# Attention and expert kernel: relu of q moved from GpSimd to VectorE one batch ahead, v scaling shared by ScalarE and VectorE, early expert reads without the last batch's writes among their dependencies

## The chip, the cores and the metric

The kernel runs on one core of a Trainium2 chip. The core has five engines, each with a queue of its own that is worked off in order: TensorE (PE in the profile, with its weight loads as PEld), VectorE (DVE), ScalarE (ACT), GpSimd (POOL) and SyncE (SP, which here only issues DMAs). Sixteen DMA engines move data between DRAM and the on-chip memory SBUF; matmul results land in PSUM. The metric is the device time in microseconds (us); less is better.

## The reference

A linear attention with cosine weights, followed by a mixture of experts with one expert per token. There are 8 batches of 8 heads, 576 positions and 64 dimensions; the attention result, turned to 4608 tokens of 512 features, is the experts' input.

```python
theta = np.pi / 2.0 * pos / S                       # S = 576
phi = lambda x: concat([relu(x) * cos(theta), relu(x) * sin(theta)])   # on the last axis
kv  = einsum('bhsf,bhsd->bhfd', phi(k), v);  z = sum(phi(k), axis=2)
attn = einsum('bhsf,bhfd->bhsd', phi(q), kv) / (einsum('bhsf,bhf->bhs', phi(q), z) + 1e-06)
x = attn.transpose(0, 2, 1, 3).reshape(4608, 512)
logits = x @ w_gate;  expert = argmax(logits);  gate = softmax(logits)[expert]   # 8 experts
# the first 1152 tokens of each expert are kept, in token order
out[i] = gate[i] * (relu(x[i] @ w1[expert]) @ w2[expert])   # w1: 512 x 1024, w2: 1024 x 512; others 0
```

## The kernel before

A batch's 576 positions are cut into `NJ` = 4 chunks of 128 and a tail of 64 (`NC` = 5); its 8 heads go in 4 pairs. The first part loops over `it` = 0 to 8 (`B` = 8) and works on three batches at a time. Each stage returns a list of small steps, and `run` merges the lists into one program: a list is given with the stretch (lo, hi) of the iteration over which its steps are spread evenly, and the steps of all lists are sorted by that place. This fixes the order in every engine's queue.

- `load(it + 1)` issues the six DMAs of the next batch on SP: k, v and q, each as a main part and a tail. k and v have two buffers, q (`qm`, `qt`) has one, so the next q can be loaded only when the relu of the present one has read it.
- `stage_a(it)`: `relu_k` on ACT; `relu_q(w)`, four instructions on POOL that write the rectified q of a head pair into `qr` with the heads reordered, and two more for the tail, `qrt`; `scale_v(c, t)`, which multiplies chunk c of v by the cosine (t = 0) or sine (t = 1) table into `vs`, on DVE for the four chunks and on ACT for the tail; `q_pair(w)`, which turns a pair of `qr` on PE (`q_ps`) and copies it to `rq` on ACT; `kv_pair(w)`, the products of k and scaled v on PE (`kv_ps`), with a copy to `kvt` on ACT and one to `kva` on DVE for every two pairs; then `transp` and `gates`, which fold the router's weights into `kva` (`t_ps`, `g_ps`).
- `stage_p(it - 1)`: ten units, each four products of `rq` and `kva` on PE (`p_ps`, two buffers), a scaled copy on ACT (`tmp`) and a multiply-add on DVE (`num`).
- `stage_r(it - 2)`: the router, about twenty small DVE instructions in one chain with an Exp on ACT (`ex`) and the counting product on PE (`c_ps`, which needs `oh`); it makes the row numbers `slot_i` and the factors `rden`. Then `emit(c)` multiplies the token rows (`xg`; chunks 1 and 3 on POOL, the rest on DVE), and `scatter(c)` writes them by indirect DMAs on POOL to `xd`, a DRAM buffer sorted by expert.
- `w1_piece(0, e)`: one expert's first half of w1 (`w1a`), a DMA on POOL near the end of an iteration. Seven of the eight go one per iteration, and the eighth beside the last.

After the loop `table_a` works out, on DVE, where the first `NA` = 24 blocks of 128 rows lie. The second part runs over 43 blocks: `fetch` reads a block from `xd` by a transposing DMA on SP (`xT`, ten buffers, and `ids`), `up` multiplies with w1 (`h_ps`), `turn` transposes, `down` multiplies with w2 (`y_ps`), and rows go to the output by an indirect DMA on POOL. The first seven blocks run `up` with `w1a` alone beside the router of the last batch (`stage_r(7)`, `table_b`); the loads of `w1b` (second half of w1) and `w_sb` (w2) follow on POOL behind that router's scatters. `down` of block 0 comes 17 blocks behind its `up` and needs all of `w_sb`.

A read of `xd` depends on the writes that stand ahead of it in the program. Writes and reads can be declared free of a group: the scatters of the last batch and the zero rows of `table_b` are free of reads that were put into "early reads" ahead of them.

## Time and profile before

| | us |
|---|---|
| median of 3 runs | 501.11 (497.33 to 501.25) |
| profiled execution, its own time | 497.33 |
| its span, first to last instruction | 495.5 |
| PE busy | 349.4 (71%) |
| POOL busy | 192.1 (39%) |
| DVE busy | 185.3 (37%) |
| ACT busy | 170.6 (34%) |

The profile is of one execution. Its span lies 1.8 us below the time of the same execution. Busy times are sums over stages with different limits, so none of them says by itself what bounds the kernel; the order of time and the waits do. An engine's wait is given with the instruction that ended it ("<-POOL qr"). PEclk is TensorE's granted clock, as a share of the full one.

### The profile page before, as it was taken

Reading aid. Unit: us, or ns where it says so; the run is one execution under the profiler, and the core shown is the slowest. Engines: PE = TensorE matmul, PEld = TensorE weight load, DVE = VectorE, ACT = ScalarE, POOL = GpSimd, SP = SyncE. Lnnn points to the kernel's source line nnn. Section 1 sums busy time; section 2 is a strip of 40 time slices with the busy share of each in tenths; the row PEclk is TensorE's granted clock in tenths of the full one; section 3 lists DMA queues with packets and bytes.
Section 4 is the critical chain, followed back from the end, with each engine's and each line's share of the span. In section 5 each row is a group of like instructions: output and inputs, shape, how many; then the busy total and the mean of one; then the engine's idle time right before and its main releaser. Section 6 shows DMA issues by size and latency. Waiting matters only on the chain.

```text
span 495.5 us, 8167 instructions
## 1 busy us (share of the span) xinstructions
PE 349.4 (71%) x2672; PEld 219.3 (44%) x2672; DVE 185.3 (37%) x544; ACT 170.6 (34%) x319; POOL 192.1 (39%) x205
## 2 busy tenths in 40 slices
PE   0099969495867859587406022987499999999994
PEld 0066657374645647366303011443155555555441
DVE  1203456445474635456836200231023232223222
ACT  1046574433645435343202000452033434333110
POOL 3163604908375573916524722000022222222544
PEclk9998979777887978787658555998799999999998
DMA  2968372828467381404173999999955433111221
GB/s 47 331 198 270 81 224 68 234 78 259 119 200 179 112 247 30 82 1 83 41 114 82 183 198 201 190 187 197 158 117 113 102 97 111 72 64 64 92 91 54
DMA packets 91559, 66.55 MB, mean 134 GB/s; under 512 B 46077, under 2 KB 88061, under 8 KB 91520
## 3 DMA queue, kind: packets, MB, share of 16 engines
q0 software_dynamic: 22000, 30.96, 28.9%
q1 hardware_dynamic: 68368, 34.01, 28.0%
q10 hardware_dynamic: 1152, 1.05, 0.7%
q8 instruction: 24, 0.39, 0.3%
q14 instruction: 15, 0.12, 0.1%
HBM read 61.92 MB, written 17.06 MB: 159 GB/s over the span
## 4 chain that ended last, share of the span: by engine, by line
PE 31%; issue 24%; POOL 19%; DMA 15%; SPq 4%; DVE 3%; ACT 2%; another core or an unknown queue 1%; POOLq 1%; ACTq 0%; DVEq 0%
PE h_ps L660 13%; PE y_ps L681 9%; POOL qr L217 7%; POOL xd L493 5%; DMA xT<-xd 5%; DMA out_dram<-y,ix 4%; DMA qm<-in_q_dram 4%; PE ht_ps L671 3%; PE kv_ps L291 2%; POOL xg L485 2%; PE p_ps L329 2%; DMA ids<-xd 2%; POOL qrt L222 2%; POOL out_dram L693 1%
## 5 line engine op out<-in xcount | busy, mean ns | idle before, releaser
L662 ACT ACTIVATE h<-h_ps 128x512 bf16<-128x512 f32 x86 | 51.4, 597 | 126.4 <-PE h_ps L660 116.4
L681 PE MATMUL y_ps<-w_sb,hT 128*128 x344 | 81.1, 384 | 8.8 <-DMA w_sb<-in_moe_w_dram 6.5
L329 PE MATMUL p_ps<-kva,rq 64*128 64x146 f32 (+1 forms) x640 | 77.0, 356 | 3.9 <-ACT kva L315 2.4
L672 DVE COPY hT<-ht_ps 128x512 bf16<-128x512 bf16 x86 | 33.2, 420 | 119.8 <-PE ht_ps L671 107.9
L660 PEld LDWEIGHTS <-xT 128*128 128x128 bf16 x344 | 34.4, 101 | 98.3 <-DMA xT<-xd 40.3
L660 PE MATMUL h_ps<-w1a,xT 128*128 x172 | 47.2, 399 | 43.1 <-DMA xT<-xd 43.0
L336 DVE SCALAR_TENSOR_TENSOR num<-p_ps,sintab,tmp 128x292 f32<-128x292 f32 (+1 forms) x80 | 41.6, 520 | 84.6 <-ACT tmp L334 83.6
L693 POOL DMA_INDIRECT out_dram<-y,ids x24 | 23.4, 977 | 121.6 <-DVE y L687 84.0
L262 PE MATMUL q_ps<-ident,qr 128*128 128x128 f32 x128 | 30.0, 377 | 53.3 <-POOL qr L217 53.3
L329 PEld LDWEIGHTS p_ps<-kva,rq 64*128 64x128 f32 (+1 forms) x640 | 56.6, 215 | 15.9 <-issue 5.6
L217 POOL TENSOR_SCALAR qr<-qm 128x512 f32<-128x512 f32 x32 | 46.8, 1485 | 30.5 <-DMA qm<-in_q_dram 30.1
L485 POOL TENSOR_TENSOR xg<-num,rden 128x512 bf16<-128x512 f32 x16 | 21.0, 1313 | 95.4 <-DVE rden L478 95.3
L660 PE MATMUL h_ps<-w1b,xT 128*128 x172 | 47.3, 401 | 15.0 <-DMA ids<-xd 14.9
L334 ACT ACTIVATE tmp<-p_ps,costab 128x292 f32<-128x292 f32 (+1 forms) x80 | 40.0, 502 | 48.8 <-PE p_ps L329 47.1
L681 PEld LDWEIGHTS <-hT 128*128 128x128 bf16 x344 | 32.9, 99 | 45.0 <-issue 12.2
L493 POOL DMA_INDIRECT xd<-xg,slot_i x40 | 42.8, 1069 | 10.0 <-issue 8.2
L262 PEld LDWEIGHTS q_ps<-ident,qr 128*128 128x128 f32 x128 | 19.3, 188 | 60.8 <-POOL qr L217 56.6
L291 PE MATMUL kv_ps<-vs,km 128*64 128x130 f32 x512 | 39.9, 303 | 0.0
L264 ACT COPY rq<-q_ps 128x512 f32<-128x512 f32 x32 | 18.6, 581 | 45.8 <-PE q_ps L262 45.7
L291 PEld LDWEIGHTS kv_ps<-vs,km 128*64 128x64 f32 x512 | 31.2, 150 | 5.8 <-issue 1.0
L687 DVE COPY y<-y_ps 128x512 f32<-128x512 f32 x22 | 15.2, 692 | 45.9 <-PE y_ps L681 24.8
L671 PEld LDWEIGHTS <-h 128*128 128x128 bf16 x344 | 24.3, 101 | 14.1 <-issue 2.7
(140 smaller groups left out, 339.7 us busy)
## 6 DMA issues: line engine op xcount, KB each, us to landing
km<-in_k_dram SPq DMA_DIRECT2D x8, 1024.0 KB
vm<-in_v_dram SPq DMA_DIRECT2D x8, 1024.0 KB
qm<-in_q_dram SPq DMA_DIRECT2D x8, 1024.0 KB
w_sb<-in_moe_w_dram POOLq DMA_DIRECT2D x8, 1024.0 KB
w1a<-in_moe_w_dram POOLq DMA_DIRECT2D x8, 512.0 KB
w1b<-in_moe_w_dram POOLq DMA_DIRECT2D x8, 512.0 KB
xd<-zrow ACTq DMA_DIRECT2D x8, 128.5 KB
kt<-in_k_dram SPq DMA_DIRECT2D x8, 128.0 KB
```

Source lines behind the costliest of these rows:

```text
L217: nc.gpsimd.tensor_scalar(out=qr[:, w, :, :, :].rearrange("p j o d -> p o j d"), in0=qm[:, u * HB + r:u * HB + r + 3:2, :, :], scalar1=0.0 ...
L262: nc.tensor.transpose(out=q_ps[:, j, :], in_=qr[:, w, j, :, :].rearrange("p o d -> p (o d)"), identity=ident[:])
L291: nc.tensor.matmul(out=kv_v[o * D:(o + 1) * D, w % 2, :, :], lhsT=lhsT, rhs=rhs, start=(c == 0), stop=(c == NC - 1))
L329: nc.tensor.matmul(out=p_ps[0:rows, o, r, 0:2 * KW], lhsT=rq[o * D:(o + 1) * D, 2 * u + r, c * P:c * P + rows], rhs=kva[o * D:(o + 1) * D, ...
L334: nc.scalar.activation(out=tmp[0:rows], in_=p_v[0:rows, :, 0:KW], func=ACT.Copy, scale=costab[0:rows, c:c + 1])
L336: nc.vector.scalar_tensor_tensor(out=num[0:rows, c, u * HB:(u + 1) * HB, :], in0=p_v[0:rows, :, KW:2 * KW], scalar=sintab[0:rows, c:c + 1] ...
L493: si = nc.gpsimd.indirect_dma_start(out=xd[:, :], out_offset=bass.IndirectOffsetOnAxis(ap=slot_i[0:rows, c:c + 1], axis=0), in_=xg[0:rows, ...
L660: nc.tensor.matmul(out=h_ps[:], lhsT=bl["xT"][:, g, :], rhs=w1h[n][:, bass.ds(e1, 1), g, :], start=(g == 0), stop=(g == G - 1))
L662: nc.scalar.activation(out=h[:], in_=h_ps[:], func=ACT.Relu)
L671: nc.tensor.transpose(out=t_ps[:, f, :], in_=bl["h", n][:, f * P:(f + 1) * P], identity=identb[:])
L672: nc.vector.tensor_copy(out=bl["hT"][:, n * (FB // 2):(n + 1) * (FB // 2), :], in_=t_ps[:])
L681: nc.tensor.matmul(out=y_ps[:], lhsT=bl["hT"][:, f, :], rhs=w2_sb[:, bass.ds(e2, 1), f, :], start=(f == 0), stop=(f == FB - 1))
```

## The change

The relu of q leaves `stage_a` and becomes a function of its own, `relu_q(b)`: four DVE instructions, two for the main part (one for each head of a pair, 1024 elements per partition) and two for the tail (256 elements). In iteration `it` it is run for batch `it + 1`, spread from 0.7 to 0.95; batch 0's stands ahead of the loop. v scaling of chunks 2 and 3 goes from DVE to ACT, and the list of scalings is written in another order. The `kva` copy goes from DVE to ACT. `stage_r` is spread over 0 to 0.85 in place of 0 to 1, and over 0 to 0.5 in the last iteration, where `table_a`, now in two pieces, takes 0.5 to 1. The eight `w1a` pieces are all issued by iteration 7, two each in iterations 6 and 7. The first 24 fetches are declared free of the "late rows": the last batch's scatters and the zero rows.

```diff
+    def relu_q(b):
+        if b >= B:
+            return []
+        qm, qt = loaded[b]["q"]
+        qr = io1.tile([P, 4, NJ, 2, D], FP32, name="qr", tag="qr")
+        qrt = io1.tile([D, 4, 2, D], FP32, name="qrt", tag="qrt")
+        qrs[b] = (qr, qrt)
+        def main(o):
+            def f():
+                nc.vector.tensor_scalar(
+                    out=qr[:].rearrange("p (u r) j o d -> p u (r j) o d", u=2)[:, :, :, o, :],
+                    in0=qm[:].rearrange("p (u o r) j d -> p u o (r j) d", u=2, o=2)[:, :, o, :, :],
+                    scalar1=0.0, scalar2=None, op0=ALU.max)
+            return f
...
+        return [main(0), main(1), tail(0), tail(1)]
...
-        def relu_q(w):
-            def f():
-                u, r = w // 2, w % 2
-                nc.gpsimd.tensor_scalar(
-                    out=qr[:, w, :, :, :].rearrange("p j o d -> p o j d"),
-                    in0=qm[:, u * HB + r:u * HB + r + 3:2, :, :], scalar1=0.0, scalar2=None, op0=ALU.max)
...
+        qr, qrt = qrs.pop(b)
...
-                if c == NJ:
+                if c >= 2:
                     nc.scalar.activation(out=vs[0:rows, c, :, t, 0:D], in_=src, func=ACT.Copy,
...
         elem += [relu_k(0)]
-        for c in range(NC):
-            elem += [scale_v(c, 0), scale_v(c, 1)]
-            if c == 1:
-                elem.append(relu_k(1))
+        elem += [scale_v(0, 0), scale_v(2, 0), scale_v(0, 1), scale_v(2, 1), relu_k(1), scale_v(1, 0),
+                 scale_v(3, 0), scale_v(1, 1), scale_v(3, 1), scale_v(4, 0), scale_v(4, 1)]
...
-                    nc.vector.tensor_copy(out=kva[:, w - 1:w + 1, :, 0:D + 1], in_=kv_v)
+                    nc.scalar.copy(out=kva[:, w - 1:w + 1, :, 0:D + 1], in_=kv_v)
...
                 if b == B - 1:
                     free_of(si, "early reads")
+                    member(si, "late rows")
...
             free_of(zi, "early reads")
+            member(zi, "late rows")
...
     load(0)
+    run((relu_q(0), 0.0, 1.0))
     for it in range(B + 1):
         streams = []
         if it < B:
             load(it + 1)
-            elem, rls, qs, kvst = stage_a(it)
-            streams += [(elem, 0.0, 0.5), (rls, 0.0, 0.3), (qs, 0.1, 0.5), (kvst, 0.45, 1.0)]
+            elem, qs, kvst = stage_a(it)
+            streams += [(elem, 0.0, 0.5), (qs, 0.0, 0.45), (kvst, 0.45, 1.0)]
+        if it + 1 < B:
+            streams.append((relu_q(it + 1), 0.7, 0.95))
         if 1 <= it:
             streams.append((stage_p(it - 1), 0.05, 0.97))
         if 2 <= it:
-            streams.append((stage_r(it - 2, ps_a, "a"), 0.0, 1.0))
-            streams.append(([w1_piece(0, it - 2)] + ([w1_piece(0, 7)] if it == B else []), 0.9, 1.0))
+            streams.append((stage_r(it - 2, ps_a, "a"), 0.0, 0.85 if it < B else 0.5))
+            if it < B:
+                lots = {6: (4, 5), 7: (6, 7)}.get(it, (it - 2,))
+                streams.append(([w1_piece(0, e) for e in lots], 0.9, 1.0))
+            else:
+                streams.append((table_a(), 0.5, 1.0))
         run(*streams)
-    table_a()
...
         if i < NA:
-            member(ti, "early reads")
-            member(di, "early reads")
+            for x in (ti, di):
+                free_of(x, "late rows")
+                member(x, "early reads")
```

What this moves in the engines' queues is shown at three places. The first is POOL in an iteration of the middle, from the router's first write of one batch (the token numbers in `xg`) on. Before:

```order
L217 TENSOR_SCALAR qr<-qm 128x2x4x64 x4
L222 TENSOR_SCALAR qrt<-qt 64x2x2x64 x2
L485 TENSOR_TENSOR xg<-num_186,rden 128x512
L493 DMA xd<-xg,slot_i 37888x514
L485 TENSOR_TENSOR xg<-num_186,rden 128x512
L493 DMA xd<-xg,slot_i 37888x514 x3
L508 DMA w1a<-in_moe_w_dram 128x4x512
L493 DMA xd<-xg,slot_i 37888x514
L374 TENSOR_SCALAR xg<-tok_i 128x5
```

And now:

```order
L384 TENSOR_SCALAR xg<-tok_i 128x5
L495 TENSOR_TENSOR xg<-num_186,rden 128x512
L503 DMA xd<-xg,slot_i 37888x514
L495 TENSOR_TENSOR xg<-num_186,rden 128x512
L503 DMA xd<-xg,slot_i 37888x514 x4
L519 DMA w1a<-in_moe_w_dram 128x4x512
```

The six relu instructions are gone from the queue, and the w1 piece stands behind the last scatter.

The second place is ACT in the first half of an iteration of the middle, up to the second scaling of v's tail (`vs<-vt,sintab`). Before:

```order
L264 COPY rq<-q_ps 128x512
L230 ACTIVATE km<-km 128x1024
L233 ACTIVATE kt<-kt 64x512
L334 ACTIVATE tmp<-p_ps,costab 128x292
L264 COPY rq<-q_ps 128x512
L334 ACTIVATE tmp<-p_ps,costab 128x292
L264 COPY rq<-q_ps 128x512
L242 ACTIVATE vs<-vt,costab 64x8x64
L273 COPY rq<-qt_ps 128x4x64
L334 ACTIVATE tmp<-p_ps,costab 128x292
L242 ACTIVATE vs<-vt,sintab 64x8x64
```

And now:

```order
L274 COPY rq<-q_ps 128x512
L242 ACTIVATE km<-km 128x1024
L245 ACTIVATE kt<-kt 64x512
L344 ACTIVATE tmp<-p_ps,costab 128x292
L254 ACTIVATE vs<-vm,costab 128x8x64
L274 COPY rq<-q_ps 128x512
L344 ACTIVATE tmp<-p_ps,costab 128x292
L254 ACTIVATE vs<-vm,sintab 128x8x64
L283 COPY rq<-qt_ps 128x4x64
L254 ACTIVATE vs<-vt,costab 64x8x64
L344 ACTIVATE tmp<-p_ps,costab 128x292
L254 ACTIVATE vs<-vt,sintab 64x8x64
```

Two scalings of v's chunk 3 have come in between the q copies; those of chunk 2 stand likewise further ahead.

The third place is DVE near the end of an iteration of the middle, from the sixth `num` on. Before:

```order
L336 SCALAR_TENSOR_TENSOR num_184<-p_ps,sintab,tmp 128x292
L478 TENSOR_TENSOR rden<-rden,gate 128x40
L485 TENSOR_TENSOR xg<-num_186,rden 128x512
L336 SCALAR_TENSOR_TENSOR num_184<-p_ps,sintab,tmp 128x292
L485 TENSOR_TENSOR xg<-num_186,rden 128x512
L295 COPY kva<-kv_ps 128x4x65
L336 SCALAR_TENSOR_TENSOR num_184<-p_ps,sintab,tmp 64x292
L485 TENSOR_TENSOR xg<-num_186,rden 64x512
L336 SCALAR_TENSOR_TENSOR num_184<-p_ps,sintab,tmp 64x292
```

And now:

```order
L346 SCALAR_TENSOR_TENSOR num_186<-p_ps,sintab,tmp 128x292
L495 TENSOR_TENSOR xg<-num_184,rden 128x512 x2
L346 SCALAR_TENSOR_TENSOR num_186<-p_ps,sintab,tmp 128x292
L214 TENSOR_SCALAR qr<-qm 128x16x64
L346 SCALAR_TENSOR_TENSOR num_186<-p_ps,sintab,tmp 128x292
L495 TENSOR_TENSOR xg<-num_184,rden 64x512
L214 TENSOR_SCALAR qr<-qm 128x16x64
L346 SCALAR_TENSOR_TENSOR num_186<-p_ps,sintab,tmp 64x292
L222 TENSOR_SCALAR qrt<-qt 64x4x64 x2
L346 SCALAR_TENSOR_TENSOR num_186<-p_ps,sintab,tmp 64x292
```

The next batch's relu of q stands between the last four `num`, and the `kva` copy is gone.

## Rows read from the trace of the kernel before

**Rows 1.** The page's chain that ended last, shares of the span by line.

```profile
PE h_ps L660 13%; PE y_ps L681 9%; POOL qr L217 7%; POOL xd L493 5%; DMA xT<-xd 5%; DMA out_dram<-y,ix 4%; DMA qm<-in_q_dram 4%; PE ht_ps L671 3%; PE kv_ps L291 2%; POOL xg L485 2%; PE p_ps L329 2%; DMA ids<-xd 2%; POOL qrt L222 2%; POOL out_dram L693 1%
```

**Rows 2.** Busy time by step; columns: us, then PE, PEld, DVE, ACT, POOL, PEclk, DMA, GB/s.

```profile
41.32:61.38 20.06, 18.94 (x193) 14.19 (x193) 8.93 (x20) 12.61 (x26) 8.11 (x8) 0.91 0.61 180
61.38:85.85 24.47, 20.23 (x205) 15.71 (x205) 14.70 (x44) 14.21 (x28) 4.95 (x4) 0.86 0.47 145
85.85:115.75 29.90, 22.35 (x205) 17.07 (x206) 15.58 (x45) 13.06 (x27) 17.06 (x16) 0.77 0.56 157
115.75:143.21 27.46, 19.73 (x205) 15.13 (x205) 14.96 (x45) 12.96 (x27) 16.63 (x15) 0.81 0.61 169
...
198.10:227.60 29.50, 21.28 (x212) 16.41 (x211) 15.72 (x47) 13.35 (x29) 17.53 (x16) 0.83 0.20 40
```

**Rows 3.** Order of time in step 4; start, us, engine, line; idle before in brackets.

```profile
120.83 5.84 POOL L217 TENSOR_SCALAR qr<-qm 128x512 f32<-128x512 f32 x4
...
122.37 1.12 PE L262 MATMUL q_ps<-ident,qr 128*128 128x128 f32 x4 [5.62 <-POOL qr L217]
...
126.64 1.81 POOL L222 TENSOR_SCALAR qrt<-qt 64x256 f32<-64x256 f32 x2
...
137.87 1.55 POOL L485 TENSOR_TENSOR xg<-num,rden 128x512 bf16<-128x512 f32 x1 [9.41 <-DVE rden L478]
```

**Rows 4.** Order of time in step 2, PE and ACT.

```profile
63.67 1.28 ACT L397 ACT_TABLE_LOAD   x1
...
69.45 0.27 PE L424 MATMUL c_ps<-oh,ub 128*128 128x32 bf16 x4 [3.91 <-DVE oh L411]
...
75.81 0.59 PE L291 MATMUL kv_ps<-vs,kt 64*64 64x130 f32 x4
```

**Rows 5.** Groups by form, 41.32 to 227.60 us; xcount, busy us and mean ns, idle before.

```profile
L334 ACT ACTIVATE tmp<-p_ps,costab 128x292 f32<-128x292 f32 x56 | 28.1, 502 | 39.8 <-PE p_ps L329 39.4
...
L264 ACT COPY rq<-q_ps 128x512 f32<-128x512 f32 x28 | 16.3, 581 | 35.0 <-PE q_ps L262 34.9
...
L230 ACT ACTIVATE km<-km 128x1024 f32<-128x1024 f32 x14 | 14.8, 1059 | 0.2
...
L245 DVE TENSOR_SCALAR vs<-vm,sintab 128x512 f32<-128x512 f32 x28 | 13.7, 489 | 0.0
...
L295 DVE COPY kva<-kv_ps 128x260 f32<-128x260 f32 x14 | 6.0, 429 | 6.5 <-ACT kvt L294 6.5
...
L242 ACT ACTIVATE vs<-vt,costab 64x512 f32<-64x512 f32 x7 | 5.1, 725 | 0.0
...
L233 ACT ACTIVATE kt<-kt 64x512 f32<-64x512 f32 x7 | 4.3, 617 | 0.0
```

**Rows 6.** Batch 0: k load issued (order of time), q landed (chain).

```profile
8.83 0.60 SPq L195 DMA_DIRECT2D km<-in_k_dram  x1
...
13.21 9.23 DMA qm<-in_q_dram
```

**Rows 7.** Order of time behind step 8's start: POOL, the DMA queue, PE.

```profile
249.60 1.01 POOL L493 DMA_INDIRECT xd<-xg,slot_i  x1 [0.30 <-issue]
...
256.18 1.31 SPq L644 DMA_TRANSPOSE xT<-xd  x1
...
261.35 0.31 PE L424 MATMUL c_ps<-oh,ub 128*128 128x32 bf16 x4
...
275.12 1.63 POOL L508 DMA_DIRECT2D w1b<-in_moe_w_dram  x2
```

**Rows 8.** PE's wait for w_sb (waits), and the chain's first y_ps.

```profile
PE y_ps L681 <- DMA w_sb<-in_moe_w_dram: 6.5, 1, 6.5
...
356.50 3.34 PE y_ps L681 x8
```

**Rows 9.** Order of time in step 8, DVE and POOL.

```profile
241.95 2.26 DVE L485 TENSOR_TENSOR xg<-num,rden 64x512 bf16<-64x512 f32 x1
242.58 1.08 POOL L485 TENSOR_TENSOR xg<-num,rden 128x512 bf16<-128x512 f32 x1
```

More of the change, by code (lines that the diff above doesn't have):

```diff
@@ L183 @@
     nc.vector.tensor_copy(out=carry[0][:], in_=base[:])
-    loaded, kvs, rqs = {}, {}, {}
+    loaded, kvs, rqs, qrs = {}, {}, {}, {}
     def load(b):
@@ L201, in head, with tail, f @@
         return (w // 2) * HB + 2 * o + w % 2
+    def relu_q(b):
[12 more added lines that the diff above has]
+            return f
+        def tail(o):
+            def f():
+                nc.vector.tensor_scalar(
+                    out=qrt[:].rearrange("p (u r) o d -> p u r o d", u=2)[:, :, :, o, :],
+                    in0=qt[:].rearrange("p (u o r) d -> p u o r d", u=2, o=2)[:, :, o, :, :],
+                    scalar1=0.0, scalar2=None, op0=ALU.max)
+            return f
+        return [main(0), main(1), tail(0), tail(1)]
     def stage_a(b):
@@ L209, in stage_a @@
         elem, qs, kvst, tail = [], [], [], []
-        qr = io1.tile([P, 4, NJ, 2, D], FP32, name="qr", tag="qr")
-        qrt = io1.tile([D, 4, 2, D], FP32, name="qrt", tag="qrt")
-        def relu_q(w):
-            def f():
-                u, r = w // 2, w % 2
-                nc.gpsimd.tensor_scalar(
-                    out=qr[:, w, :, :, :].rearrange("p j o d -> p o j d"),
-                    in0=qm[:, u * HB + r:u * HB + r + 3:2, :, :], scalar1=0.0, scalar2=None, op0=ALU.max)
-                if w == 3:
-                    for uu in range(2):
-                        nc.gpsimd.tensor_scalar(
-                            out=qrt[:, 2 * uu:2 * uu + 2, :, :].rearrange("p r o d -> p o r d"),
-                            in0=qt[:, uu * HB:(uu + 1) * HB, :].rearrange("p (o r) d -> p o r d", o=2),
-                            scalar1=0.0, scalar2=None, op0=ALU.max)
-            return f
+        qr, qrt = qrs.pop(b)
         def relu_k(u):
@@ L315, in gates @@
                 nc.scalar.copy(out=kva[o * D:(o + 1) * D, :, :, D + 1:KW], in_=g_v[o * D:(o + 1) * D, :, :, o, :])
-        return elem, [relu_q(w) for w in range(4)], qs, kvst + [transp, gates]
+        return elem, qs, kvst + [transp, gates]
     def stage_p(b):
@@ L579, in table_a, with f, g @@
     def table_a():
-        full = whole("a", False)
-        tbl, incl, _ = table("a", NA, full[:], None, False)
-        tabs["a"] = tbl
-        done = tp.tile([P, E], FP32, name="done")
-        nc.vector.tensor_tensor(out=done[:], in0=incl[:], in1=full[:], op=ALU.subtract)
-        nc.vector.tensor_scalar(out=done[:], in0=done[:], scalar1=-1.0, scalar2=float(NA * P), op0=ALU.mult,
-                                op1=ALU.add)
-        nc.vector.tensor_scalar(out=done[:], in0=done[:], scalar1=0.0, scalar2=None, op0=ALU.max)
-        nc.vector.tensor_tensor(out=done[:], in0=done[:], in1=full[:], op=ALU.min)
-        tabs["done"] = done
+        def f():
+            full = whole("a", False)
+            tabs["full"] = full
+            tabs["a"], tabs["incl"], _ = table("a", NA, full[:], None, False)
+        def g():
+            full, incl = tabs["full"], tabs["incl"]
+            done = tp.tile([P, E], FP32, name="done")
+            nc.vector.tensor_tensor(out=done[:], in0=incl[:], in1=full[:], op=ALU.subtract)
+            nc.vector.tensor_scalar(out=done[:], in0=done[:], scalar1=-1.0, scalar2=float(NA * P), op0=ALU.mult,
+                                    op1=ALU.add)
+            nc.vector.tensor_scalar(out=done[:], in0=done[:], scalar1=0.0, scalar2=None, op0=ALU.max)
+            nc.vector.tensor_tensor(out=done[:], in0=done[:], in1=full[:], op=ALU.min)
+            tabs["done"] = done
+        return [f, g]
     def table_b():
```

## The prediction

> **What bounds the kernel now.** I read the chain that ended last first. It has three stretches: attention, a middle in which the expert weights come in, and a matmul stretch from 356 us to the end. The chain's shares by line put the relu of q on POOL (qr, qrt) at 9% [rows 1], and all of it lies in the first 228 us. So I cut that stretch at the first p_ps product of each batch and took the busy times of each piece. A piece is called a step; step 1 starts at 41.32 us and step 8 at 227.60 us. The steps are very unequal [rows 2]: step 1 takes 20.06 us, step 2 takes 24.47, step 3 29.90, steps 4 to 6 27.46 each (one is shown), step 7 29.50. No engine fills them: in step 4 PE is busy 19.73, POOL 16.63, DVE 14.96, ACT 12.96, and the DMA engines hold 0.61 of it.
>
> The order of time inside step 4 gives the reason [rows 3]. POOL starts the relu of q at 120.83, and the first transpose waits on it for 5.62 us; PE has nothing else, since its queue is in order. POOL was not free earlier: it was issuing the row scatters of the batch before. After relu and tail (5.84 + 1.81) POOL sits idle for 9.41 us until rden is ready, multiplies xg, scatters, and only then reaches the next relu. So the loop goes relu on POOL, transposes and products on PE, router on DVE, scatters on POOL, relu. Steps 1 and 2 lie ahead of that loop: there q was ready, and PE did not wait for POOL. They show what a step costs without it.
>
> **The change, part by part.**
>
> *Relu of q from POOL to DVE, one batch ahead.* It takes 7.65 us per batch out of POOL's queue [rows 3], where it was in the loop. On DVE it is four instructions. There is no row for 1024 elements on DVE: from below, the same kind of instruction takes 0.489 us for 512 elements [rows 5], so 0.98 for a main one; from above, POOL's own rate, 1.46 us per 512, gives 2.92. I take 0.98, the same operation on the same engine, and at most 0.49 for a tail: 2.9 us per batch. DVE gives up four v scalings (4 x 0.489) and two kva copies (2 x 0.429) [rows 5], 2.8 us, so its sum stays at about 15 of a step; it does not set the end. The cover is its idle time behind num in the second half of a step; without cover it would be 2.9 us per step.
>
> *v scaling of columns 2 and 3, and the kva copy, to ACT.* Four scalings at 0.725 and two copies at about 0.43 [rows 5], 3.8 us per step. This is the part that costs, since with q ready the first half of a step is set by ACT's queue: PE may end its first kv pair only behind the second v tail scaling. Up to there ACT now has two km relus (1.059), kt (0.617), five q copies (0.581 at most), five tmp (0.502) and six scalings (0.725): 2.12 + 0.62 + 2.91 + 2.51 + 4.35 = 12.5 us. I leave the overlap of neighbours in, against the wait for dl in front of Exp. In step 2 the same point came 14.43 us into the step (75.81 - 61.38) [rows 4], with 1.28 us of table load that comes once, and with PE waiting 3.91 us for oh. From that point to the next step it took 10.04 us (85.85 - 75.81). With one kva copy now ahead of a tmp, 0.43: the new step is 12.5 + 10.04 + 0.43 = **23.0 us**. Bounds: step 1 (20.06: no router, no POOL wait) and step 2 (24.47: router and table load, no POOL wait).
>
> So steps 2 to 7 go from 166.2 us (227.60 - 61.38) to 6 x 23.0 = 138.0: **28.2 us gained**; 45.9 by the lower bound, 19.4 by the upper.
>
> The Trainium skill says, in "ScalarE: Activation LUTs", Rules for kernel authors, that max and mul belong on VectorE and not on ScalarE. The trace agrees on the single instruction, 0.725 against 0.489 us [rows 5]. By that rule alone the split costs 4 x 0.24 = 0.9 us per step and the sum below would be 5.7 us worse than one without the split; the 12.5 us above hold the whole of it already.
>
> *The first two batches.* In step 1 PE did not wait for POOL, so the split only costs: 12.5 + 10.0 = 22.5 without the Exp wait and its DVE chain, which I round down to 22.1, against 20.06: **2.0 us lost** (0 to 2.9, four scalings). Batch 0 I hold even: q lands at 22.44 us [rows 6], relu then takes 2.9 on DVE where POOL took 1.46 to the first pair, but all pairs are ready together.
>
> *Order in step 8, the tables, the w1 pieces.* Now the last rows of batch 6 are issued at 249.60, 22.0 us into step 8; the first xT read follows at 256.18, the router product of batch 7, which PE has queued behind the first expert product, at 261.35, and the first w1b load at 275.12 [rows 7], 47.5 us into the step. After the change batch 6's router ends by the middle of the step and two w1a issues are no longer between the scatters. I put the last issue at about 18, and the same distances behind it give a w1b load at 43.5; the table's DVE work no longer stands ahead of batch 7's router, which gives another 1.5. **5.5 us gained** (0 to 8).
>
> *Early reads freed of the late rows.* The reads of blocks 6 to 8 no longer wait for the last scatters and the zero rows, and go ahead of the weight stream. That stream decides: PE waited 6.5 us for w_sb before its first y_ps [rows 8], so PE could use at most 6.5 us. The stream's length is its bytes; only the reads taken out of it shorten it. **2 us** (0 to 6.5). Everything behind the first y_ps at 356.50, 139 us of the span, has the same instructions [rows 8].
>
> **Sum.** 28.2 - 2.0 + 5.5 + 2 = 33.7 us against the profiled execution: 497.33 us (span 495.5 and 1.8 around it). 497.3 - 33.7 = 463.6, forecast **463 us**. The median of the runs, 501.11, lies 3.8 above that execution; I leave that in the range.
>
> **The rivals.**
>
> *Steps like step 2.* The chain tmp, num, oh, c_ps holds PE as it did in step 2 (3.91 us), with a lower granted clock behind it (0.86 there, 0.91 in step 1 [rows 2]). 6 x 24.5: 28.2 becomes 19.3, so 473 us. For it: that step had the router and no POOL wait. Against it: 1.28 of it was a table load.
>
> *Faster.* If PE, no longer idle 5.6 us per step, keeps the higher clock and ACT's neighbours overlap, a step is near step 1, 20 to 21 us. 6 x 20.5 gives 15 us more: 448 us. Against it: step 1 has no router.
>
> *DVE and POOL in each other's way.* In step 8 a DVE multiply of 512 elements took 2.26 us, and did not end before POOL's own multiply (1.08) that began 0.63 us behind it [rows 9]. A relu of q that meets POOL's xg could wait as long as that takes, 1.08 to 1.55 us [rows 3, 9]; where one or two of them a step hold up num, six steps cost 9 to 18 us: 472 to 481 us. It decides once DVE's idle time behind num is used up. The Trainium skill has the rule behind it: in "SBUF — State Buffer", Who interferes with whom, a VectorE copy or tensor_scalar in a two-port mode and a GpSimd instruction exclude each other for a whole instruction. The 2.26 us row bears it out for a two-input multiply; no row of this trace shows it for a scatter's issue.
>
> *Slower: q lands too late.* The relu of the next q now stands in DVE's queue ahead of three num, so if q is late, num, p_ps and the next step wait. With L from the km issue to q's landing, the next step starts about 4 us behind L (relu, num, p_ps, gate product, kva), and km is issued 3 us ahead of a step: the step is at least L + 1. Now L is 13.6 us (8.83 to 13.21 + 9.23) [rows 6], and the DMA work of a whole step is 0.61 x 27.46 = 16.7 us [rows 2]. It decides from L of about 22, and is slower than before only from 27. At L = 30, 6 x 31 is 20 us more than now: 497 + 20 - 7.5 = 510 us. Nothing in the rows comes near.
>
> *No gain.* Something else in the loop, such as POOL's scatters behind rden, keeps the step at 27.5: 28.2 is gone and 492 to 499 us are left. Against it: POOL keeps 9 us of work in 27.
>
> **How the numbers follow.** Chances: my forecast 0.53 (own range 455 to 470), like step 2 0.15, DVE against POOL 0.08, faster 0.17, no gain 0.04, slower 0.03. The range 448 to 478 leaves out about half of the faster case and half of the DVE case and the last two, 0.2 in all. About 1%, 5 us, is what a measurement of this kernel tells from no change: faster by more than that 0.93, within it 0.04, slower 0.03.
>
> **What would show it.** Right: no q_ps product waits for a relu, steps 2 to 7 are within 22 to 24 us, ACT is busy about 17 us in each and is what kv waits for (vs), POOL idles between its scatters; the first w1b load comes about 42 us into step 8; the stretch from the first y_ps to the end is 139 us again. Wrong: num waits behind qr for qm, or a DVE relu takes over 1.5 us; steps of 24.5 or more with c_ps waiting for oh; a first y_ps that still comes about 129 us behind the start of step 8, as now.

## The result and the profile after

The changed kernel takes 467.82 us (median, 466.35 to 468.2); the kernel before ran at 499.22 beside it. The ratio is 0.9372, 95% interval 0.9306 to 0.9438: faster, inside the predicted range, 4.8 us above the forecast of 463. In this document medians and ranges leave out executions more than 1.5% above the fastest of the same version on the same chip. The profiled execution has a span of 466.2 us, 29.3 less than before.

The chain's shares by line, from the page of the changed kernel, answer to [rows 1]: POOL's `qr` and `qrt` have left it.

```profile
PE h_ps L683 13%; PE kv_ps L301 10%; PE y_ps L704 10%; PE p_ps L339 8%; DMA xT<-xd 7%; DMA w1b<-in_moe_w_dram 5%; DMA out_dram<-y,ix 4%; PE ht_ps L694 3%; DVE num L346 2%; ACT vs L254 2%; PE q_ps L272 2%; ACT tmp L344 2%; DMA qm<-in_q_dram 2%; PE g_ps L322 2%; DMA qt<-in_q_dram 2%
```

Busy time by step of the changed kernel, the answer to [rows 2]; columns: us, then PE, PEld, DVE, ACT, POOL, PEclk, DMA share, GB/s. A step is again the stretch between the first p_ps products of two batches.

```profile
43.43:63.83 20.40, 17.85 (x193) 13.56 (x192) 8.26 (x19) 14.92 (x31) 0.00 (x0) 0.94 0.54 165
63.83:86.84 23.01, 19.59 (x206) 15.61 (x205) 15.71 (x43) 16.73 (x34) 6.59 (x6) 0.85 0.55 163
86.84:111.36 24.52, 21.70 (x206) 16.97 (x206) 14.40 (x43) 15.54 (x33) 10.09 (x11) 0.79 0.70 185
111.36:134.06 22.70, 19.87 (x206) 15.72 (x206) 15.55 (x43) 15.55 (x33) 8.09 (x9) 0.85 0.77 206
...
180.74:204.71 23.97, 18.38 (x203) 14.33 (x202) 13.36 (x41) 15.34 (x33) 11.50 (x14) 0.93 0.42 79
```

Steps 2 to 7 now take 22.7 to 24.5 us, 23.5 on average (23.0 was forecast), where they took 24.5 to 29.9. POOL's work falls from 16.63 to 8.09 us in step 4, ACT's rises from 12.96 to 15.55.

Order of time in step 4 of the changed kernel, the answer to [rows 3] and [rows 4].

```profile
117.70 0.27 PE L434 MATMUL c_ps<-oh,ub 128*128 128x32 bf16 x4 [2.77 <-DVE oh L421]
...
122.94 0.73 ACT L254 ACTIVATE vs<-vt,sintab 64x512 f32<-64x512 f32 x1
...
123.97 0.55 PE L301 MATMUL kv_ps<-vs,kt 64*64 64x130 f32 x4
124.40 1.05 POOL L495 TENSOR_TENSOR xg<-num,rden 128x512 bf16<-128x512 f32 x1 [11.45 <-DVE rden L488]
...
127.74 1.12 POOL L503 DMA_INDIRECT xd<-xg,slot_i  x1 [2.29 <-DVE xg L495]
...
128.34 2.17 DVE L214 TENSOR_SCALAR qr<-qm 128x1024 f32<-128x1024 f32 x1
...
128.88 1.08 POOL L495 TENSOR_TENSOR xg<-num,rden 128x512 bf16<-128x512 f32 x1
...
131.47 0.70 DVE L214 TENSOR_SCALAR qr<-qm 128x1024 f32<-128x1024 f32 x1
```

In steps 2 to 7 no product waits for a relu of q any more. In step 4 the first half, up to the tail product behind the second v-tail scaling, is 123.97 - 111.36 = 12.61 us (12.5 forecast), the rest 10.09 (10.47). PE's one long wait in a step is for `oh`, 2.77 us here. PE's waits for it and for `vs` in all of steps 2 to 7 (us in total, times, longest):

```profile
PE c_ps L434 <- DVE oh L421: 17.0, 6, 3.2
PE kv_ps L301 <- ACT vs L254: 0.9, 2, 0.8
```

So the 12.61 us have the forecast length, but PE waits in them for DVE's `oh`; it hardly waits for ACT's `vs`, which the prediction named.

### The profile page after: what moved, and what is told of

It is laid out like the page before. It is cut to its first block, busy times and chain, and to the rows that moved or that the text cites. A ratio compares the mean times of both kernels' runs of the same rounds, so it can differ in the third digit from the quotient of the medians.

```text
span 466.2 us, 8117 instructions
## 1 busy us (share of the span) xinstructions
PE 344.4 (74%) x2651; PEld 219.6 (47%) x2672; DVE 182.4 (39%) x528; ACT 191.6 (41%) x367; POOL 130.0 (28%) x157
## 4 chain that ended last, share of the span: by engine, by line
PE 49%; DMA 20%; DVE 8%; issue 7%; ACT 7%; POOL 3%; SPq 3%; another core or an unknown queue 1%; POOLq 0%; DVEq 0%; ACTq 0%
PE h_ps L683 13%; PE kv_ps L301 10%; PE y_ps L704 10%; PE p_ps L339 8%; DMA xT<-xd 7%; DMA w1b<-in_moe_w_dram 5%; DMA out_dram<-y,ix 4%; PE ht_ps L694 3%; DVE num L346 2%; ACT vs L254 2%; PE q_ps L272 2%; ACT tmp L344 2%; DMA qm<-in_q_dram 2%; PE g_ps L322 2%; DMA qt<-in_q_dram 2%
## 5 line engine op out<-in xcount | busy, mean ns | idle before, releaser
L339 PE MATMUL p_ps<-kva,rq 64*128 64x146 f32 (+1 forms) x640 | 75.2, 353 | 8.8 <-DVE num L346 6.8
L683 PEld LDWEIGHTS <-xT 128*128 128x128 bf16 x344 | 34.4, 101 | 72.3 <-issue 28.2
L339 PEld LDWEIGHTS p_ps<-kva,rq 64*128 64x128 f32 (+1 forms) x640 | 55.0, 212 | 22.5 <-DVE num L346 12.5
L495 POOL TENSOR_TENSOR xg<-num,rden 128x512 bf16<-128x512 f32 x16 | 18.0, 1128 | 144.3 <-DVE rden L488 144.1
L683 PE MATMUL h_ps<-w1b,xT 128*128 x168 | 45.1, 391 | 16.8 <-issue 16.6
L503 POOL DMA_INDIRECT xd<-xg,slot_i x40 | 44.3, 1108 | 22.7 <-DVE xg L495 13.7
L301 PE MATMUL kv_ps<-vs,km 128*64 128x130 f32 x512 | 43.7, 322 | 1.7 <-ACT vs L254 1.7
L272 PE MATMUL q_ps<-ident,qr 128*128 128x128 f32 x128 | 25.1, 334 | 23.4 <-DVE qr L214 23.4
L694 PE MATMUL ht_ps<-identb,h 128*128 128x128 bf16 x344 | 28.4, 224 | 14.3 <-ACT h L685 14.3
L301 PEld LDWEIGHTS kv_ps<-vs,km 128*64 128x64 f32 x512 | 34.3, 162 | 8.2 <-issue 4.8
L708 ACT COPY y<-y_ps 128x512 f32<-128x512 f32 x21 | 12.3, 587 | 48.6 <-DMA out_dram<-y,ix 25.1
L272 PEld LDWEIGHTS q_ps<-ident,qr 128*128 128x128 f32 x128 | 17.7, 172 | 25.9 <-issue 23.7
```

The costliest lines, as they stand in the source:

```text
L272: nc.tensor.transpose(out=q_ps[:, j, :], in_=qr[:, w, j, :, :].rearrange("p o d -> p (o d)"), identity=ident[:])
L301: nc.tensor.matmul(out=kv_v[o * D:(o + 1) * D, w % 2, :, :], lhsT=lhsT, rhs=rhs, start=(c == 0), stop=(c == NC - 1))
L339: nc.tensor.matmul(out=p_ps[0:rows, o, r, 0:2 * KW], lhsT=rq[o * D:(o + 1) * D, 2 * u + r, c * P:c * P + rows], rhs=kva[o * D:(o + 1) * D, ...
L503: si = nc.gpsimd.indirect_dma_start(out=xd[:, :], out_offset=bass.IndirectOffsetOnAxis(ap=slot_i[0:rows, c:c + 1], axis=0), in_=xg[0:rows, ...
L683: nc.tensor.matmul(out=h_ps[:], lhsT=bl["xT"][:, g, :], rhs=w1h[n][:, bass.ds(e1, 1), g, :], start=(g == 0), stop=(g == G - 1))
L694: nc.tensor.transpose(out=t_ps[:, f, :], in_=bl["h", n][:, f * P:(f + 1) * P], identity=identb[:])
```

## The experiments

The program is cut at three points for all of them: the start of step 2, the start of step 8, the first y_ps. These four stretches, from windows of one profiled execution of each version, are the measure of each part:

| us | before | relu_only | no_split | changed | router_early |
|---|---|---|---|---|---|
| up to step 2 | 61.38 | 56.43 | 58.02 | 63.83 | 58.30 |
| steps 2 to 7 | 166.22 | 148.93 | 129.56 | 140.88 | 119.22 |
| step 8 to first y_ps | 128.90 | 130.04 | 121.92 | 119.49 | 106.38 |
| first y_ps to the end | 139.0 | 139.2 | 141.7 | 142.0 | 143.6 |

The versions below ran on four chips. The kernel before, run beside them, had medians of 498.6 to 501.8 us there, so a few us between versions of different chips tell nothing. One execution against another of the same instructions can differ by more in a stretch: steps 2 to 7 of the changed kernel took 140.88 us here and 140.08 in a second profile (after_again); in reads_wait and step8_before, whose steps 2 to 6 hold the same instructions, they took 133.50 and 133.48.

### The relu alone, and the change without the split

relu_only is the kernel before, plus the new `relu_q` and these lines:

```diff
-            streams += [(elem, 0.0, 0.5), (rls, 0.0, 0.3), (qs, 0.1, 0.5), (kvst, 0.45, 1.0)]
+            streams += [(elem, 0.0, 0.5), (qs, 0.0, 0.45), (kvst, 0.45, 1.0)]
+        if it + 1 < B:
+            streams.append((relu_q(it + 1), 0.7, 0.95))
```

> The kernel before with one part of the change alone: the relu of q and of its tail runs on DVE one batch ahead, with the places in the order that the changed kernel gives them; v scaling, kva copies, the order of step 8, the w1 pieces and the early reads stay as before. Theory (the loop through POOL was the whole cost): steps 2 to 7 fall from 27.7 us to about 23.2 (step 2 of before, 24.47, without its one table load of 1.28), so 27 us are gained, nothing is lost in the first two batches, and the time is about 472 us. Rival 1 (the split is what made ACT the clean pace; without it DVE, which now has relu, v scaling and kva copies, holds up num and oh): steps of 25 us or more, 483 us or more, with c_ps waiting longer for oh than the 2.8 us it waits in the changed kernel. Rival 2 (POOL's scatters bound the loop anyway): steps stay above 27, 495 us.

Measured: 476.38 us (474.52 to 481.55), where the kernel before had 495.04 and 502.23 on the same chip. That lies between the theory and the first rival: steps 2 to 7 take 24.8 us on average, and c_ps waits 4.1 us a step for `oh`. no_split is the changed kernel with this edit (and the order of the list as before):

```diff
-                if c >= 2:
+                if c == NJ:
...
-                    nc.scalar.copy(out=kva[:, w - 1:w + 1, :, 0:D + 1], in_=kv_v)
+                    nc.vector.tensor_copy(out=kva[:, w - 1:w + 1, :, 0:D + 1], in_=kv_v)
```

> The changed kernel with v scaling (all but the tail) and the kva copies back on DVE, in the order of before; the rest as changed. Theory of the prediction (ACT's queue paces the first half of a step, 12.5 us up to the second v-tail scaling; measured 12.61 in step 4): four scalings of 0.72 leave that queue, so if nothing else takes over the first half falls by up to 2.9 us and steps 1 to 7 by 2 us or more: 453 us. By the rule on ScalarE (0.24 us for each scaling, 4 a step): 462 us. Rival (DVE is the next limit: its queue holds num, the router and now 4 x 0.48 of scaling more in the same half, so oh comes later than it does now and PE waits for it, 2.8 us a step now): steps of 23.5 to 24.5, 471 to 478 us, slower than the changed kernel. I hold the rival likelier, since step 2 of the kernel before, without split and without a POOL wait, needed 13.15 us to the same point (14.43 less the table load).

Measured: **451.35 us** (449.54 to 452.95). The rival that I held likelier fell: without the split the kernel is faster by 16.5 us than the changed one, near the first theory's 453. Steps 2 to 7 of relu_only and of no_split, windows, same columns as above:

```profile
56.43:205.36 148.93, 118.36 (x1228) 93.07 (x1227) 108.19 (x284) 78.56 (x158) 52.95 (x49) 0.84 0.55 154
```

```profile
58.02:187.58 129.56, 114.03 (x1227) 90.29 (x1226) 102.51 (x284) 77.97 (x158) 56.02 (x52) 0.89 0.67 183
```

ACT is busy for about the same in both and DVE for 5.7 us less, and yet no_split is 19.4 us shorter. The waits of PE in these stretches (us in total, times, longest), first relu_only, then no_split, say where:

```profile
PE c_ps L436 <- DVE oh L423: 24.8, 6, 4.6
PE q_ps L274 <- DVE qr L214: 3.8, 5, 0.9
```

```profile
PE c_ps L436 <- DVE oh L423: 14.6, 6, 2.4
```

These waits differ by 14.0 us, and PE's own busy time by 4.3, at granted clocks of 0.84 and 0.89.

Against the changed kernel, no_split's step 4 reaches the tail product 134.01 - 122.83 = 11.18 us into the step instead of 12.61, and needs 9.99 behind it instead of 10.09:

```profile
122.83 0.90 PE L341 MATMUL p_ps<-kva,rq 64*128 64x146 f32 x8
...
128.82 0.25 PE L436 MATMUL c_ps<-oh,ub 128*128 128x32 bf16 x4 [2.42 <-DVE oh L423]
...
134.01 0.44 PE L303 MATMUL kv_ps<-vs,kt 64*64 64x130 f32 x4
```

In this pair of executions the split costs 11.3 us in steps 2 to 7 and 5.8 before them. Other executions price it lower. With the split, reads_wait has this for steps 2 to 7:

```profile
63.22:196.72 133.50, 113.79 (x1228) 89.75 (x1227) 89.87 (x248) 94.14 (x194) 51.63 (x52) 0.90 0.65 178
```

Without it, w1b_first and zeros_late have 129.79 and 131.70 us there, and 57.56 and 58.12 before step 2, where the four executions with the split have 63.22 to 64.54. So the split costs 1.8 to 11.3 us in steps 2 to 7 and 5.1 to 7.0 before them. At one granted clock, 0.92, a middle step takes 21.2 to 21.4 us in no_split and 21.8 to 22.3 in reads_wait; the rest is a clock that differs between executions.

The rows point to a way through DVE. The waits of `num` for `tmp` in steps 2 to 7, first the changed kernel, then no_split:

```profile
DVE num L346 <- ACT tmp L344: 44.4, 44, 2.2
```

```profile
DVE num L348 <- ACT tmp L346: 23.4, 25, 1.8
```

With the scalings among the `tmp` in ACT's queue DVE waits longer for `tmp`, `oh` stands behind `num` in DVE's queue, and PE's wait for `oh` is 2.77 us in steps 3 to 7 of the changed kernel where it is 2.42 to 2.44 in no_split. In all six steps that is 2.4 us; what else makes up the cost is not shown.

### How the router is spread

What sets no_split apart from relu_only in the middle is the stretch over which the router's instructions are spread. router_late is no_split with that one number as before:

```diff
-            streams.append((stage_r(it - 2, ps_a, "a"), 0.0, 0.85 if it < B else 0.5))
+            streams.append((stage_r(it - 2, ps_a, "a"), 0.0, 1.0 if it < B else 0.5))
```

> The version without the split (no_split, span 451.2, steps of 21.2 to 22.3 us) with one number changed: in the steps in which attention still runs, the router's instructions are spread over the whole iteration again (0.0 to 1.0 as before the change, not 0.0 to 0.85). Theory (this spread, which the prediction counted for step 8 only, is a large part of the gain in the middle: oh comes earlier and PE waits less for it): steps of 24 to 25 us as in relu_only, which differs from no_split in the middle by this spread, and about 3 us a step back: 467 to 471 us. Rival (relu_only is slow for its w1 pieces or by its chip): steps stay at 21 to 22, 452 us.

Measured: 469.46 us (468.06 and 470.85), as the theory has it. Steps 2 to 7 take 149.18 us in all, as in relu_only, and the long wait is back (router_late, waits of PE in these steps):

```profile
PE c_ps L436 <- DVE oh L423: 25.5, 6, 4.6
```

The spread is worth 149.18 - 129.56 = 19.6 us (19.4 against w1b_first, on the same chip as router_late), more than the relu's own 17.3 (166.22 - 148.93).

### The engine or the place

pool_ahead leaves the relu one batch ahead but on POOL (`nc.vector` back to `nc.gpsimd` in `relu_q`):

> The changed kernel with one word changed: the relu of q, still one batch ahead and at the same places in the order, runs on POOL. Tells the engine from the place. Theory (the loop is broken only if relu leaves POOL's queue, because there it stands among the scatters, behind the xg that waits for rden): POOL's second half of a step holds 7.65 us of relu beside 9 us of xg and scatters, the next q_ps waits for qr again, steps of 27 us or more, 490 to 500 us. Rival (one batch ahead is what counts, the engine does not): POOL sits idle 11 us a step, the relu fits in, steps stay at 23 and the time at 468 us.

Measured: 490.65 us (489.02 to 491.48), 22.8 more than the changed kernel and within the theory's range; steps 2 to 7 take 156.40 us, 26.1 on average. One of its steps, then POOL in it, then PE's wait:

```profile
122.02:148.64 26.62, 21.75 (x207) 16.49 (x206) 15.10 (x38) 15.52 (x32) 15.63 (x14) 0.82 0.60 151
```

```profile
134.18 1.05 POOL L495 TENSOR_TENSOR xg<-num,rden 128x512 bf16<-128x512 f32 x1 [7.79 <-DVE rden L488]
...
140.79 2.82 POOL L214 TENSOR_SCALAR qr<-qm 128x1024 f32<-128x1024 f32 x1
143.78 1.05 POOL L503 DMA_INDIRECT xd<-xg,slot_i  x1 [0.18 <-issue]
144.87 2.80 POOL L214 TENSOR_SCALAR qr<-qm 128x1024 f32<-128x1024 f32 x1
```

```profile
PE q_ps L272 <- POOL qr L214: 19.5, 5, 4.7
```

POOL is idle for 7.79 us and then has relu and scatters one behind the other. dve_own does the opposite: DVE, but in the batch's own iteration.

```diff
-            streams.append((relu_q(it + 1), 0.7, 0.95))
+            streams += [(rls, 0.0, 0.1), (elem, 0.0, 0.5), (qs, 0.1, 0.5), (kvst, 0.45, 1.0)]
```

> The changed kernel with the relu of q on DVE at the start of its own batch's iteration, not one batch ahead. Theory (the engine is what counts): DVE does the two main relus in 1.4 us and the tails in 0.5 at the start of a step, the first q_ps waits about 1 to 2 us of them, 7 to 14 us in all: 472 to 482 us. Rival (the place is what counts, because DVE's queue at that point holds the last num of the batch before and the router's first steps): steps back to 26 or more, 488 us or more.

Measured: 468.4 us (465.87 to 469.54), the changed kernel's time and below both forecasts. DVE does a main relu in 0.68 us, and in steps 2 to 7 PE has no wait for it. So the engine is what counts: "one batch ahead" shows no gain in the total. A small one is not ruled out, since at clocks of 0.92 and 0.93 steps 2 to 6 take 22.3 to 23.7 us here and 21.7 to 22.9 in the executions of the changed kernel. The relu's durations (ns: min, median, max) in dve_own and in the changed kernel:

```profile
L214 DVE TENSOR_SCALAR qr<-qm x16: 673/678/695, 22.1 to 179.6; 128x1024 f32<-128x1024 f32 x16
```

```profile
L214 DVE TENSOR_SCALAR qr<-qm x16: 680/700/2420, 22.0 to 178.1; 128x1024 f32<-128x1024 f32 x16
```

### Scalings or copies

v_dve puts only the scalings of chunks 2 and 3 back on DVE (`c >= 2` to `c == NJ`), and leaves the kva copies and the new order.

> The changed kernel with the v scalings of chunks 2 and 3 back on DVE, but with the kva copies left on ACT and the list in its new order: which half of the split costs the 17 us between dve_own or the changed kernel (467 to 468) and no_split (451). Theory (the scalings stand in the half of a step that ACT paces and, in batch 0, behind the q copies; the kva copies stand in the other half, where ACT has idle time): 451 to 454 us. Rival (each takes its share of ACT's time, 2.9 and 0.8 us a step): 455 to 458 us.

Measured: 457.59 us (453.81 to 458.14), in the rival's range. The ratio to the kernel before, 0.915 (0.9017 to 0.9283), is clear of the changed kernel's 0.9372 but not of no_split's 0.904 (0.8873 to 0.9206). So the scalings carry most of the split's cost; whether copies and order keep any of it is not settled.

### Step 8 and the early reads

step8_before takes back the end of attention:

```diff
-            streams.append((stage_r(it - 2, ps_a, "a"), 0.0, 0.85 if it < B else 0.5))
-            if it < B:
-                lots = {6: (4, 5), 7: (6, 7)}.get(it, (it - 2,))
-                streams.append(([w1_piece(0, e) for e in lots], 0.9, 1.0))
-            else:
-                streams.append((table_a(), 0.5, 1.0))
+            streams.append((stage_r(it - 2, ps_a, "a"), 0.0, 0.85 if it < B else 1.0))
+            streams.append(([w1_piece(0, it - 2)] + ([w1_piece(0, 7)] if it == B else []), 0.9, 1.0))
```

> The changed kernel with the end of attention as before: batch 6's router spread over all of the last iteration, the first expert table after it, one w1a piece an iteration and two in the last. Prices the term that the prediction put at 5.5 us (0 to 8); the traces show the first w1b load 39.5 us into step 8 instead of 47.5, and 119.5 us from step 8 to the first y_ps instead of 128.9. Theory (the weight stream is at its rate, so its start sets the first y_ps): w1b 46 to 48 us into the step, first y_ps 126 to 128 us behind it, 475 us. Rival (the early reads did it, the order nothing): 468 us.

reads_wait takes back the early reads' freedom (the line `free_of(x, "late rows")` is gone).

> The changed kernel with the reads of the early blocks waiting for the last scatters and the zero rows again, as before. Prices the term put at 2 us (0 to 6.5). Theory (the stream's bytes set the first y_ps, and these reads are inside it either way): the reads of the last early blocks land after w1b's first pieces, the first y_ps moves by 1 to 2 us, 468 to 470 us. Rival (PE then runs the first half of those blocks behind w1b's arrival and ends later): up to 6 us, 474 us.

Measured on one chip: step8_before 468.9 us (467.84 to 470.79), reads_wait 462.05 (457.93 to 464.69). The second is below both of its forecasts; the first has its rival's time. In the profile of step8_before it is the theory that holds all the same: from step 8 to the first y_ps it needs 129.96 us, as the kernel before (128.90), and its total stays low because steps 2 to 7 took 133.48 us in it where the changed kernel's first profile has 140.88. Its w1b loads start 245.4 - 197.44 = 48.0 us into the step, in the changed kernel 244.21 - 204.71 = 39.5. Both rows, step8_before first (the tile's instructions: ns, first and last start), then the changed kernel:

```profile
L519 POOL DMA_DIRECT2D w1b<-in_moe_w_dram x8: 745/802/842, 245.4 to 252.7; - x8
```

```profile
244.21 6.08 POOL L519 DMA_DIRECT2D w1b<-in_moe_w_dram  x8
```

For reads_wait that stretch is 122.18 us, so with the reads waiting the new order is still 7.8 us ahead of step8_before in it, and 6.9 in the totals, on one chip. Kernels with the reads freed have 119.49 (changed), 121.92 (no_split) and 121.94 (dve_own), so the freed reads are worth 0.2 to 2.7 us; with one execution of each, more can't be told. That reads_wait as a whole was below the changed kernel's 467.82 on another chip asked for a control:

> The changed kernel itself, once more, on the chip of the two versions beside it. Its first profile had steps of 22.7 to 24.5 us at granted clocks of 0.79 to 0.86 in most of them; reads_wait and step8_before, whose steps 2 to 6 hold the same instructions, had 21.8 to 22.9 us, mostly at 0.92. Theory (the clock that PE is granted behind its wait for oh differs from one execution to the next, and is worth 1 to 2 us a step): the time lies between 458 and 468 us, and steps at 0.92 are 22 us long again. Rival (the difference came from the reads): 467 to 468 us and steps of 23.5.

Measured: 466.92 us (464.97 to 468.3), so the size of the result stands. It ran on a third chip, so it does not settle why reads_wait was faster, and its time fits the theory and, within 0.1 us, the rival. For the theory: in this one execution step 3 took 21.75 us at a clock of 0.92 and step 5, with the same instructions, 25.21 at 0.80. Behind the first y_ps it needs 139.5 us where the first profile needed 142.0, with the same instructions.

### Versions that follow from it

w1b_first is no_split with the w1b loads ahead of the last batch's scatters (`0.65, 1.0` to `0.0, 0.02` for them).

> The version without the split (451 us) with w1b's loads issued on POOL ahead of the last batch's scatters instead of behind them. In the changed kernel's trace DMA is busy 0.3 from the start of step 8 to the first w1b load and 0.98 from there to the first y_ps 80 us later. Theory (the stream runs at its rate and its start sets the first y_ps; the memory is free once the last tmp is read, 20 us ahead of today's first load): the first y_ps and the end come 15 to 19 us earlier, 432 to 436 us. Rival (the early reads and the scatters of the last batch now queue in the stream, PE gets its first blocks late and the first half of the experts slides behind w1b): 445 us or more.

Measured: 444.79 us (443.63 to 446.59). The load came 20 us earlier, the first y_ps only 7.5 (114.45 behind step 8 instead of 121.92): the rival's time. Order of time, ACT and then PE:

```profile
241.02 16.27 ACTq L616 DMA_DIRECT2D xd<-zrow  x8
257.40 1.09 ACT L687 ACTIVATE h<-h_ps 128x512 bf16<-128x512 f32 x2 [22.74 <-DMA xd<-zrow]
```

```profile
258.05 1.10 PE L696 MATMUL ht_ps<-identb,h 128*128 128x128 bf16 x8 [14.64 <-ACT h L687]
259.63 2.72 PE L685 MATMUL h_ps<-w1b,xT 128*128 x6 [0.48 <-DMA w_sb<-in_moe_w_dram]
```

ACT issues eight zero-row writes, 16.27 us in which the relu of h stands behind them. Each issue lasts about 0.35 us; the trace has seven of the eight starting within 0.03 us of the landing of an `xT` or `ids` read, on whose completion semaphore they wait. Those reads land late in the loaded stream (the first of the seven, issued at 226.44 us, landed at 241.0), so the rival's late reads are in the cause. zeros_late moves those issues to POOL behind w_sb (`nc.scalar.dma_start` to `nc.gpsimd.dma_start`, after the w_sb loop):

> The version w1b_first (444.8 us) with the eight zero-row writes moved from ACT's queue, where their issue took 16.3 us and the last relu of h stood behind it, to POOL behind the last w_sb load. In w1b_first PE waited 14.6 us for that relu, with w1b there since 237 us. Theory: PE starts the second half of the first blocks at about 244 instead of 259.6, the first y_ps comes 8 to 13 us earlier, 432 to 437 us. Rival (the xT reads of the next blocks, which queue in the weight stream, or the stream's own end hold PE next): no more than 4 us, 440 us or more.

Measured: 444.16 us (440.24 to 445.77). In the profiles that stretch fell as the theory says, from 114.45 to 105.68 us, and the span by 5.0 (443.6 to 438.6), with steps 2 to 7 1.9 us and the end 1.3 us longer. The medians, from two chips, hardly differ, as the rival has it; where the rest of the 8.8 us went in the other executions stays open. In the profile the first y_ps now waits 4.5 us for a zero-row write, since POOL issues these one by one as the w_sb pieces land. router_early then draws the router's first ten instructions together:

```diff
-            streams.append((stage_r(it - 2, ps_a, "a"), 0.0, 0.85 if it < B else 0.5))
+            rs = stage_r(it - 2, ps_a, "a")
+            if it < B:
+                streams += [(rs[:10], 0.0, 0.12), (rs[10:], 0.27, 0.85)]
+            else:
+                streams.append((rs, 0.0, 0.5))
```

> zeros_late with the router's first ten instructions (up to oh and the sum behind it) drawn together at the start of each iteration and the router's products left where they stand in PE's queue, so that oh is there when PE comes to c_ps. Theory (PE waits 2.4 us a step for oh and runs at the low clock behind it; with both gone the first half of a step is ACT's 10 us): steps of 19.5 to 20.3 us instead of 21.2 to 22.3, 7 to 10 us less than zeros_late. Rival (num, which now stands behind the router on DVE, holds up PE's p_ps instead): steps of 21 us or more, no gain.

Measured: **429.11 us** (427.57 to 430.54), ratio to before 0.857 (0.8505 to 0.8634), below both kernels and 15 us below zeros_late, more than the theory's 7 to 10. Steps 2 to 7, windows:

```profile
58.30:177.52 119.22, 104.75 (x1227) 80.09 (x1226) 102.53 (x283) 75.45 (x158) 55.42 (x53) 1.00 0.73 200
```

PE no longer waits for `oh` in them; 19.9 us a step at a granted clock of 1.00.

## Why the prediction was right, and where it was right by accident

The sum made of terms, each against the two profiles:

| term | predicted | measured |
|---|---|---|
| steps 2 to 7 | 28.2 gained | 25.3 (166.22 - 140.88) |
| first two batches | 2.0 lost | 2.45 lost (61.38 to 63.83) |
| step 8: order, tables, early reads | 5.5 + 2 gained | 9.4 (128.90 - 119.49) |
| behind the first y_ps | 0 | 3.0 lost (139.0 to 142.0) |
| sum | 33.7 | 29.3 |

- **What bounds: the loop through POOL.** Right. Taking the relu out of POOL's queue alone gives 17.3 us in steps 2 to 7 and 5.0 before them (relu_only), and leaving it there ahead of time gives steps of 26.1 on average (pool_ahead). That the relu's place counts too is not shown: dve_own has the same time. The rows cut step 7 of the kernel before at 198.10, where its first p_ps stands at 199.01; the sum over steps 2 to 7 does not change by it.
- **The relu on DVE.** Priced at 0.98 us, twice the row for 512 elements; it takes 0.68 to 0.70 alone.
- **The step of 23.0 us.** The step that failed, though the number held. It took 12.5 us for ACT's queue and the second half from step 2 of the kernel before, and so left out that the router's spread changes inside the steps too; that edit was counted for step 8 alone. It is worth 19.6 us in steps 2 to 7. Against it the split costs 1.8 to 11.3 there, 11.3 in the execution of the table. By the relu alone, steps would be 24.8 us, the rival "like step 2" (24.5). Two terms that the sum did not size, 19.6 and up to -11.3, stand behind the near hit, and that is luck.
- **The split's price.** ACT's queue was named as the pace of the first half, with PE waiting for `vs` and ACT busy about 17 us a step. ACT is busy 15.3 to 16.7, PE waits 0.9 us for `vs` in all six steps and 17.0 for `oh`; so the 12.5 us came out with another wait in them. The prediction's 0.24 us for each scaling, 5.7 us in all, is below what the split costs up to step 8: 17.1 (11.3 + 5.8) in the pair above, 6.9 to 17.4 between all executions with and without it. Four scalings of 0.72 and two copies of 0.39 entered ACT's queue, 3.7 us a step; 1.9 of it came out as time in that pair, where four differences of 0.24 make 0.96. The Trainium skill's rule in "ScalarE: Activation LUTs", Rules for kernel authors, that mul and max go to VectorE, held for this change, and more strongly than I weighed it.
- **The first two batches.** The sum is right, and again two terms stand behind it: by the relu on DVE alone 5.0 us are gained up to step 2 (relu_only), which the prediction put at nothing, and the split takes 5.1 to 7.0. The places change with the execution: batch 0 loses 2.11 us (held even) and step 1 loses 0.34 (2.0) in this profile, 1.07 and 2.09 in after_again. In batch 0 the new scalings on ACT stand behind q copies that wait for q, and PE waits 4.2 us for `vs` up to step 2 (1.8 in no_split).
- **Step 8.** Right, and undersized: the order alone takes w1b from 47.5 to 39.5 us into the step (42 forecast), and step8_before gives all of it back in its stretch. Freed reads: within the bounds, at most 2.7.
- **139 us behind the first y_ps.** 142.0 in this profile, 139.5 in the next of the same kernel, so the spread between executions covers the 3.0 us.
- **DVE and POOL in each other's way.** The sign came, 2.17 us for a relu that met POOL's `xg`, but no price shows: dve_own, where none is above 0.70, has the same time. The rule cited from the Trainium skill, "SBUF — State Buffer", Who interferes with whom, is borne out for a one-input max of 1024 elements: 2.17 us beside POOL's multiply, which ended at 129.96, against 0.70 alone. That relu began inside POOL's scatter issue (127.74 to 128.86) and ended at 130.51, 0.55 us behind the multiply; whether the issue held it as well is not settled. The 2.26 us row that the prediction set beside the rule is of a two-input multiply, which the rule as quoted does not cover.
- **q too late, no gain:** neither came; the only two waits of a relu for `qm` (18.52 and 7.08 us) lie ahead of step 1.
- **The signs.** No q_ps waits for a relu in the steps, and w1b's first load came even before its 42 us. Of the signs of being wrong two came in part: step 3 took 24.52 us with c_ps waiting for `oh`, and relus took up to 2.42 us. Both belong to rivals, and the time was right beside them.

## What to carry to other kernels

An instruction moved to another engine can cost more than the difference of its two durations, so price a move by the queue that it enters, by what stands behind it there and by who waits for that. Price every changed number in each stage in which it acts: here one spread counted for the end of a loop did most of its work inside it. And when a sum comes out right, take its parts away one by one: two large terms had cancelled in part, and leaving out the one with the wrong sign gave 16.5 us more. Before a stretch of one execution is compared with another's, compare two executions of the same instructions: here two of them differed by 5.5 us over steps 2 to 6 (116.9 and 111.4).
